# Result rows 4 partitions apart, one output DMA, stationary operands padded to 32 columns: a decode block on one core

## The chip, the cores and the metric

The kernel runs on one core of a Trainium2 chip. The metric is the device time of an execution in microseconds (us); the tables quote medians. The profile is one execution taken by the hardware profiler; its span is about 2.1 us shorter than the time quoted.

## The reference

The block is one decode step for 8 sequences of width 512. It attends over the last 1024 positions of a key/value cache (32 query heads, 8 key/value heads of 128), runs a gated FFN, and gates the attention result with it.

```
xn = layernorm(x)                                    # x: 8 x 512, bf16
q  = xn @ wq;  k, v = last 1024 rows of the caches
s  = softmax(q k^T / sqrt(128)) v  @ wo              # 8 x 512
g  = silu((gelu(xn @ w_gate) * (xn @ w_up)) @ w_down)
return x + s * g
```

## The kernel before

All caches and weights, 47.46 MB, are streamed through 21 slots of 1 MB by SyncE's DMA queue. The computation runs under that stream. The result is kept as 128 partitions x 128 columns: column tile q (128 of the 512 columns) lies on partitions 32 q to 32 q + 7, one row per sequence. The four tiles are made by four column groups of TensorE.

```
for q in range(NQ):                                  # residual, 4 loads of 2 KB
    nc.scalar.dma_start(out=xq_sb[32*q : 32*q+B, :], in_=x_flat[:, q*P : (q+1)*P])
...
nc.vector.memset(s_ps, 0.0)
...
def project_out(m):
    for e in range(HS):
        for q in range(NQ):
            nc.tensor.matmul(s_ps[32*q : 32*q+B, :], oE[m][:, e, :],   # 8 columns
                             wo_t[m][:, e, q*P : (q+1)*P], ...)
...
for m in range(NM):
    project_out(m)
nc.vector.tensor_tensor(out=tmp, in0=s_ps, in1=g_sb, op=ALU.mult)
nc.vector.tensor_tensor(out=out_sb, in0=tmp, in1=xr_sb, op=ALU.add)
for q in range(NQ):                                  # result, 4 stores of 2 KB
    eng = nc.sync if q % 2 == 0 else nc.scalar
    eng.dma_start(out=out_flat[:, q*P : (q+1)*P], in_=out_sb[32*q : 32*q+B, :])
```

The framework gives each DMA one of eight semaphores, taken in turn over all queues (called HW0 to HW7 here). A DMA waits until the previous user of its semaphore has landed.

The softmax here doesn't subtract the row's maximum and nothing guards it: scores larger than these inputs give would overflow.

## Time and profile before

| | before |
|---|---|
| time, median | 123.18 us (123.14 to 123.26, 3 runs) |
| span of the profile | 121.1 us |
| last projection group starts | 116.75 us |
| out_sb ready | 118.44 us |
| fourth output DMA landed | 120.29 us |
| from out_sb to the end of the span | 2.70 us |

These are lines of the page of the kernel before. The DMA row has the busy tenths of the DMA engines in 40 slices of the span. The last line is the share of each engine in the chain of work that ended last.

```profile
span 121.1 us, 4123 instructions
DMA  3999999999999999999999999999999999999820
DMA 82%; PE 12%; DVE 2%; SPq 1%; issue 0%
```

DMA is the limit from slice 2 to slice 37. What comes before the first transfer or after the last one can still give something, and the change acts mostly at the end. The timeline shows the end (start, duration, engine, line, instruction, and in brackets the idle time before it with what ended it); SPq and ACTq are the issuing of DMAs on SyncE and ScalarE.

```profile
116.75 1.02 PE L383 MATMUL s_ps<-slot,oE_2360 128*8 128x128 bf16 x32 [0.88 <-DMA slot<-in_A_wo_dram]
117.82 0.29 DVE L483 TENSOR_TENSOR tmp<-s_ps,g_sb 128x128 f32<-128x128 f32 x1 [7.06 <-PE s_ps L383]
118.14 0.29 DVE L485 TENSOR_TENSOR out_sb<-tmp,xr_sb 128x128 bf16<-128x128 f32 x1
118.47 0.71 SPq L488 DMA_DIRECT2D out_dram<-out_sb  x2
118.47 0.65 ACTq L488 DMA_DIRECT2D out_dram<-out_sb  x2
```

The view of one tile, here the output in DRAM, has the durations of the issues (minimum/median/maximum in ns).

```profile
L488 SPq DMA_DIRECT2D out_dram<-out_sb x2: 298/333/368, 118.5 to 118.9; - x2
L488 ACTq DMA_DIRECT2D out_dram<-out_sb x2: 302/306/309, 118.5 to 118.8; - x2
```

### The profile page before, as it was taken

The numbers are of one execution on the slowest core, as the hardware profiler recorded it, in microseconds if no ns is written. First come the engines' busy times: TensorE is split into PE (matmuls) and PEld (weight loads), VectorE is DVE, ScalarE is ACT, GpSimd is POOL, SyncE is SP. The second block draws the span as 40 slices with busy tenths as digits, with TensorE's granted clock in tenths as the row PEclk, the third lists the DMA queues.
The fourth block names the chain that finished last, engine by engine and source line by source line (L and its number), as shares of the span: only waits on it lengthen the run. The fifth ranks groups of instructions, "written<-read, shape, count | busy, mean of one in ns | idle before, by whom it ended". The sixth has DMA issues, their size and how long they took to land.

```text
span 121.1 us, 4123 instructions
## 1 busy us (share of the span) xinstructions
PE 86.0 (71%) x1856; PEld 71.1 (59%) x1856; DVE 72.3 (60%) x150; ACT 22.6 (19%) x70; POOL 2.4 (2%) x15
## 2 busy tenths in 40 slices
PE   0075269696875968999997969566798789955450
PEld 0061029586865957999896969565698542134340
DVE  2352046866956749678989987747798670562000
ACT  0440000321303301212330330303033300300000
POOL 6100000000000000000000000000000000000000
PEclk9999756999999985559999999999999756995555
DMA  3999999999999999999999999999999999999820
GB/s 84 387 430 430 430 427 417 419 430 425 425 427 427 425 414 422 430 419 430 425 427 422 422 417 430 422 425 422 425 433 418 422 414 434 416 430 423 341 88 5
DMA packets 6929, 47.73 MB, mean 394 GB/s; under 512 B 888, under 2 KB 896, under 8 KB 1920
## 3 DMA queue, kind: packets, MB, share of 16 engines
q1 hardware_dynamic: 6800, 47.46, 93.7%
q8 instruction: 14, 0.23, 0.7%
q10 hardware_dynamic: 112, 0.02, 0.1%
q14 instruction: 3, 0.02, 0.1%
HBM read 47.46 MB, written 0.01 MB: 392 GB/s over the span
## 4 chain that ended last, share of the span: by engine, by line
DMA 82%; PE 12%; DVE 2%; SPq 1%; issue 0%
DMA slot<-in_A_k_cache_dram 44%; DMA slot<-in_B_w_gate_dram 16%; DMA slot<-in_A_wo_dram 15%; DMA slot<-in_A_wq_dram 7%; PE kT_ps L282 7%; PE m_ps L329 2%; PE sc_ps L294 2%; SPq L91 1%; PE s_ps L383 1%; DVE kT L286 1%; PE m_ps L316 1%; DVE sums L318 1%; SPq L103 0%; PE m_ps L370 0%; DVE tmp L483 0%
## 5 line engine op out<-in xcount | busy, mean ns | idle before, releaser
L286 DVE COPY kT<-kT_ps 128x1024 bf16<-128x1024 bf16 x64 | 42.2, 677 | 18.1 <-PE kT_ps L282 17.5
L282 PE MATMUL kT_ps<-ident,slot 128*128 128x128 bf16 x512 | 43.4, 234 | 9.9 <-DMA slot<-in_A_k_cache_dram 9.5
L282 PEld LDWEIGHTS <-slot 128*128 128x128 bf16 x512 | 32.6, 104 | 13.3 <-DMA slot<-in_A_k_cache_dram 10.1
L304 ACT ACTIVATE pT<-sc_ps,diag 128x128 bf16<-128x128 f32 x64 | 18.2, 368 | 70.6 <-PE sc_ps L294 70.6
L294 PE MATMUL sc_ps<-qT_all,kT 128*128 128x16 bf16 x512 | 22.9, 171 | 0.3 <-issue 0.3
L329 PE MATMUL m_ps<-pT,slot 128*128 128x16 bf16 x512 | 21.8, 170 | 1.2 <-issue 1.1
L329 PEld LDWEIGHTS <-slot 128*128 128x128 bf16 x512 | 18.6, 97 | 4.6 <-issue 3.1
L294 PEld LDWEIGHTS <-kT 128*128 128x128 bf16 x512 | 20.4, 99 | 0.0
L318 DVE TENSOR_REDUCE sums<-m_ps 128x16 f32<-128x512 f32 x16 | 10.9, 684 | 1.2 <-PE m_ps L316 1.2
L402 PE MATMUL m_ps<-slot,xpT_sb 128*32 128x512 bf16 x32 | 7.7, 1105 | 0.0
L316 PE MATMUL m_ps<-pT,ones_pp 128*128 128x512 bf16 x16 | 6.7, 416 | 0.7 <-ACT pT L304 0.7
L250 PE MATMUL m_ps<-slot,xnT_sb 128*32 128x512 bf16 x32 | 3.5, 527 | 4.2 <-DMA slot<-in_A_wq_dram 4.2
L234 PE MATMUL m_ps<-ident,xhat 8*128 8x8 bf16 x4 | 0.3, 168 | 7.0 <-DVE xhat L214 7.0
L259 DVE CAST q_sb<-m_ps 128x512 bf16<-128x512 f32 x2 | 1.3, 686 | 6.6 <-PE m_ps L250 6.6
L356 DVE TENSOR_TENSOR wide<-m_ps,hmask 64x1024 bf16<-64x1024 bf16 x4 | 4.9, 1216 | 0.5 <-PE m_ps L352 0.4
L483 DVE TENSOR_TENSOR tmp<-s_ps,g_sb 128x128 f32<-128x128 f32 x1 | 0.3, 292 | 7.1 <-PE s_ps L383 7.1
L250 PEld LDWEIGHTS <-xnT_sb 128*32 128x32 bf16 x32 | 0.8, 101 | 6.2 <-issue 5.8
L322 DVE RECIPROCAL recip<-sums 128x16 f32<-128x16 f32 x16 | 4.0, 253 | 0.6
L234 PEld LDWEIGHTS <-xhat 8*128 8x128 bf16 x4 | 0.2, 102 | 7.0 <-DVE xhat L214 7.0
L402 PEld LDWEIGHTS <-xpT_sb 128*32 128x32 bf16 x32 | 1.7, 117 | 4.3 <-issue 3.4
L338 DVE TENSOR_TENSOR oT_all<-m_ps,recip 128x16 bf16<-128x16 f32 x16 | 3.5, 218 | 0.4 <-PE m_ps L329 0.3
L352 PE MATMUL m_ps<-ident,oT_all 128*64 128x128 bf16 x4 | 1.0, 253 | 2.7 <-DVE sums L318 2.1
(71 smaller groups left out, 33.4 us busy)
## 6 DMA issues: line engine op xcount, KB each, us to landing
slot<-in_A_k_cache_dram SPq DMA_DIRECT2D x16, 1024.0 KB, 19.4
slot<-in_A_v_cache_dram SPq DMA_DIRECT2D x16, 1024.0 KB, 19.7
slot<-in_A_wq_dram SPq DMA_DIRECT2D x4, 1024.0 KB, 8.6
slot<-in_A_wo_dram SPq DMA_DIRECT2D x3, 1024.0 KB, 18.0
slot<-in_B_w_gate_dram SPq DMA_DIRECT2D x2, 896.0 KB, 20.0
slot<-in_B_w_up_dram SPq DMA_DIRECT2D x2, 896.0 KB, 18.9
slot<-in_B_w_down_dram SPq DMA_DIRECT2D x2, 896.0 KB
slot<-in_A_wo_dram SPq DMA_DIRECT2D x1, 768.0 KB, 17.7
```

What stands on the lines that cost most here:

```text
L250: nc.tensor.matmul(q_ps[n][Q * q : Q * (q + 1), :], xnT_sb[:, k, :], wq_t[k][:, hkv * NW : (hkv + 1) * NW], start=(k == 0), stop=(k == NDC ...
L282: nc.tensor.transpose(t_ps[:, c * P : (c + 1) * P], k_t[g][:, cc * Dh : (cc + 1) * Dh], ident)
L286: nc.vector.tensor_copy(out=kT[n], in_=t_ps)
L294: nc.tensor.matmul(sc[g][:, s * CB + c, :], kT[n][:, c * P : (c + 1) * P], qT_all[:, hkv, b0 : b0 + I, :], start=True, stop=True,)
L304: nc.scalar.activation(out=pT[g][:, :, i * rep : (i + 1) * rep], in_=sc[g][:, :, i * rep : (i + 1) * rep], func=ACT.Exp, bias=diag[:, i : ...
L316: nc.tensor.matmul(sums_ps, ones_pp, pT[g], start=True, stop=True)
L318: nc.vector.tensor_reduce(out=sums, in_=sums_ps.rearrange("p c m -> p m c"), axis=AX.X, op=ALU.add)
L322: nc.vector.reciprocal(out=recip[g], in_=sums)
L329: nc.tensor.matmul(oT[g], v_t[g][:, c * Dh : (c + 1) * Dh], pT[g][:, c, :], start=(c == 0), stop=(c == C - 1),)
L338: nc.vector.tensor_tensor(out=oT_all[:, hkv * rep : (hkv + 1) * rep, b0 : b0 + I].rearrange("p j i -> p i j"), in0=oT[g].rearrange("p (i j ...
L356: nc.vector.tensor_tensor(out=wide, in0=t_ps.rearrange("p (q e) -> p e q", e=HS) .unsqueeze(2) .to_broadcast([HS * B, HS, HS, DQ]), in1=hm ...
L402: nc.tensor.matmul(gu_ps[w][Q * q : Q * (q + 1), :], xpT_sb[:, k, :], cols[:, j0[q] : j0[q] + JQ, :], start=(k == 0), stop=(k == NDC - 1), ...
```

## The change

The intent: four output DMAs land one behind the other, so put the 32 result rows at equal distances (sequence b of tile q on partition 32 q + 4 b), where one access pattern reaches them all. For that the stationary operands become 32 columns wide, with zeros between the valid ones. Padded matmuls write all 128 partitions, so two PSUM memsets fall away. The four small loads of the residual become one as well. (The diff is cut: context lines and the old place where oE was made are left out.)

```diff
+    QB = Q // B                                       # 32 // 8 = 4
-    for q in range(NQ):
-        nc.scalar.dma_start(
-            out=xq_sb[32 * q : 32 * q + B, :], in_=x_flat[:, q * P : (q + 1) * P]
-        )
+    nc.scalar.dma_start(out=xq_sb[::QB, :], in_=x_flat.rearrange("b (q n) -> q b n", n=P))
-    nc.vector.memset(s_ps, 0.0)
-        nc.vector.tensor_copy(out=xpT_sb[:, :, 0:B], in_=t[:, 1])
+        nc.vector.tensor_copy(out=xpT_sb[:, :, ::QB], in_=t[:, 1])
+    oE = [persist.tile([P, HS, Q], BF16, name=f"oE{m}") for m in range(NM)]
+    for m in range(NM):
+        nc.gpsimd.memset(oE[m], 0.0)
-        nc.vector.tensor_copy(out=oE[m], in_=e_ps)
+        nc.vector.tensor_copy(out=oE[m][:, :, ::QB], in_=e_ps)
-                    s_ps[32 * q : 32 * q + B, :],
+                    s_ps[Q * q : Q * (q + 1), :],
-        nc.vector.memset(f_ps, 0.0)
-                    f_ps[Q * q : Q * q + B, :],
-                    hT_sb[:, j - j0[r], Q * r : Q * r + B],
+                    f_ps[Q * q : Q * (q + 1), :],
+                    hT_sb[:, j - j0[r], Q * r : Q * (r + 1)],
-    for q in range(NQ):
-        eng = nc.sync if q % 2 == 0 else nc.scalar
-        eng.dma_start(
-            out=out_flat[:, q * P : (q + 1) * P], in_=out_sb[32 * q : 32 * q + B, :]
-        )
+    nc.sync.dma_start(
+        out=out_flat.rearrange("b (q n) -> q b n", n=P), in_=out_sb[::QB, :]
+    )
```

More of the change, by code (lines that the diff above doesn't have):

```diff
@@ L345, in value_block @@
             )
-    oE, wide_t = {}, {}
+    wide_t = {}
+    oE = [persist.tile([P, HS, Q], BF16, name=f"oE{m}") for m in range(NM)]
+    for m in range(NM):
+        nc.gpsimd.memset(oE[m], 0.0)
     def expand_out(m):
@@ L376, in select_out @@
             )
-        oE[m] = persist.tile([P, HS, B], BF16, name=f"oE{m}")
-        nc.vector.tensor_copy(out=oE[m], in_=e_ps)
+        nc.vector.tensor_copy(out=oE[m][:, :, ::QB], in_=e_ps)
     def project_out(m):
```

## The prediction

> **What bounds the kernel now.** The stream of weights and caches. The 40-slice table shows DMA at nine tenths from slice 2 to 37, at about 425 GB/s; the chain that ended last is 82% DMA, 12% PE, 2% DVE. Only what comes before the first transfer or after the last one can shorten the 121.1 us span. The timeline of the end: the last wo piece lands and starts the last 32 output-projection matmuls at 116.75 us; DVE's tmp starts at 117.82, out_sb ends at 118.44; four 2 KB output DMAs are issued, two on SP (the second at 118.88) and two on ACT, each 0.3 to 0.37 us. The trace's semaphore events show them landing one behind the other: the first complete by 119.68, the second by 119.89, the third by 120.09, the fourth by 120.29. About 0.8 us of closing barrier follows.
>
> **What the change does.**
>
> 1. Output: four DMAs become one. The first of the four needed 1.21 us from issue to landing; the fourth came 0.61 us later, about 0.2 us per DMA, whichever queue issued them. (The Trainium skill, "DMA: Bandwidth & Descriptors", section "Issuing engines are not separate DMA queues", says the queues share the same 16 engines; the trace agrees.) The same page, section "Why a DMA increments its semaphore by 16 and not by 1", says that the slowest dimensions of both patterns decide how many engines work. The old DMAs used 8 (ACT's queue has 112 packets: seven DMAs of 8 data and 8 semaphore packets); the new one, 4 x 8 rows, should use 4, each with 8 rows in series. A 256-byte packet took 15 to 21 ns, so I add 7 x 18 = 0.13 us, and up to 0.1 us for a longer issue. Estimated landing: about 119.85, 0.35 to 0.5 us earlier, all on the critical path.
>
> 2. Stationary operands of 32 columns instead of 8, in both down projections (output, FFN). In the last group the matmuls start in bursts of four, 107 ns apart at the halved clock; their weight loads start within 10 ns and lie under the running burst. Single loads took 82 ns (8 columns) and 92 ns (32 columns, query projection). I expect the spacing to remain 107 ns, and under 0.05 us of critical path. Earlier groups have over 1.4 us of slack (waits on wo).
>
> 3. Removed: two PSUM memsets on DVE (0.17 us each). Added: four GpSimd memsets (estimated 0.3 us each, GpSimd idle). Changed: a strided oE copy (0.21 us). All off the path.
>
> 4. Input: four xq DMAs (1.37 us on ACT's queue) become one, so the Sqrt and the first PE work come up to 1 us earlier. DMA semaphores come from a pool of eight taken in turn; three fewer early users let the fourth wq load and K's second load issue without waiting. But the DMA share is already about 1 from 3 us on, so a deeper queue moves 0 to 0.1 us.
>
> **Sum.** 123.18 - 0.4 gives 122.8 us, range 122.4 to 123.2. Faster by over 2%: 0.01; within 2%: 0.98; slower: 0.01.
>
> **What would show it.** One output issue on SP, out_sb's end to span end about 2.25 us instead of 2.65; the last projection group still 1.02 us; the last wo wait ending near 116.7; wq issues in one run at the start.
>
> **What would make it wrong.** The four-engine write costing more; 32-column loads spreading the bursts (up to +0.5 us); the last transfers, where throughput falls to about 150 GB/s from 115 to 116.75 us because some engines lag, ending at another time because of the changed early queue.

## More of the kernel before

At the end SyncE waits for the last count of every semaphore, in a fixed order: HW2; HW3 and HW1; HW4 and HW0; HW5; HW6; HW7, each of the last three together with an engine's semaphore. Then come a drain and a barrier.

The view of waits on SyncE's queue says for how long its closing list waited for outputs (total, times, longest):

```profile
SPq L516 <- DMA out_dram<-out_sb: 0.7, 3, 0.4
```

## The result, and the profile after

| | before | after |
|---|---|---|
| time, median | 123.21 us (4 runs) | 123.88 us (123.84 to 123.92, 4 runs) |
| ratio | | 1.0055 (95% interval 1.0038 to 1.0072) |
| span | 121.1 us | 121.8 us |
| last projection group starts | 116.75 us | 116.73 us |
| out_sb ready | 118.44 us | 118.44 us |
| last output landing | 120.29 us | 120.26 us |
| from out_sb to the end of the span | 2.70 us | 3.34 us |

A ratio is the mean time of one kernel's fast runs over that of the other's of the same rounds, so it is not quite the ratio of the medians quoted. The result is within 2%, and clearly slower by 0.5%. It lies outside the predicted range of 122.4 to 123.2 us.

The page after, same three lines as before:

```profile
span 121.8 us, 4119 instructions
DMA  3999999999999999999999999999999999999710
DMA 93%; SPq 2%; PE 1%; issue 0%; DVE 0%
```

The timeline of the end, the tile view of the output, and the wait of the closing list:

```profile
116.73 1.04 PE L384 MATMUL s_ps<-slot,oE 128*32 128x128 bf16 x32 [0.99 <-DMA slot<-in_A_wo_dram]
117.82 0.29 DVE L483 TENSOR_TENSOR tmp<-s_ps,g_sb 128x128 f32<-128x128 f32 x1 [7.27 <-PE s_ps L384]
118.14 0.29 DVE L485 TENSOR_TENSOR out_sb<-tmp,xr_sb 128x128 bf16<-128x128 f32 x1
118.46 0.69 SPq L486 DMA_DIRECT2D out_dram<-out_sb  x1
```

```profile
L486 SPq DMA_DIRECT2D out_dram<-out_sb x1: 689/689/689, 118.5 to 118.5; - x1
```

```profile
SPq L514 <- DMA out_dram<-out_sb: 1.0, 1, 1.0
```

From the start of the last projection group (116.75 and 116.73 us) to out_sb (118.44 us) the two traces agree to 0.02 us. Earlier stages differ (the FFN's down projection starts at 108.52 and 107.75 us), but all wait for the same stream. The whole difference, 0.64 us of the span, comes after the last computing instruction. The single issue takes 0.69 us where the first one took 0.37, and only one wait for an output remains.

These views do not show what SyncE does after that wait. The trace's records of SyncE's own instructions and of the semaphore events do. "n" is the place of the instruction among all of SyncE's in the trace, "gap" the time since the end of the one ahead:

```
before                                        after
 n  start    gap ns  waits for                 n  start    gap ns  waits for
78  119.219     45   HW2                       77  119.209     56   HW2
79  119.278     42   HW3, HW1                  78  119.268     42   HW3, HW1 (output; held to 120.281)
80  119.726    420   HW4, HW0 (output)         79  120.324     43   HW4, HW0
81  119.903    149   HW5 (output)              80  120.795    443   HW5
82  120.106    175   HW6 (output)              81  120.879     56   HW6
83  120.308    174   HW7 (output)              82  120.949     42   HW7
84  120.378     42   drain                     83  121.021     44   drain
output landings: 119.68 119.89 120.09 120.29   output landing: 120.26
```

Before, the outputs happen to signal on HW4 to HW7, the end of the list, and SyncE drains 0.09 us after the last landing. After, three fewer loads at the start have turned the pool of semaphores, and the output signals on HW1, in the second wait. Four more waits follow the landing, with a pause of 0.44 us before the 80th instruction although what it waits for landed long ago. The drain comes 0.76 us after the landing. From drain to the end of the span it is about 0.76 us in both kernels (121.14 - 120.38; 121.78 - 121.02).

The sum: the landing came 0.03 us earlier, the path from landing to drain grew by 0.67 us (0.76 - 0.09), together 0.64 us, which is the difference of the spans.

### The profile page after: what moved, and what is told of

Same layout as the page of the kernel before. It is cut to its first block, busy times and chain, and to the rows that moved or that the text cites. A ratio compares the mean times of both kernels' runs of the same rounds, so it can differ in the third digit from the quotient of the medians.

```text
span 121.8 us, 4119 instructions
## 1 busy us (share of the span) xinstructions
PE 87.1 (72%) x1856; PEld 71.6 (59%) x1856; DVE 72.6 (60%) x148; ACT 22.6 (19%) x70; POOL 3.4 (3%) x19
## 4 chain that ended last, share of the span: by engine, by line
DMA 93%; SPq 2%; PE 1%; issue 0%; DVE 0%
DMA slot<-in_A_k_cache_dram 62%; DMA slot<-in_B_w_gate_dram 16%; DMA slot<-in_A_wo_dram 15%; SPq L106 2%; PE s_ps L384 1%; SPq L94 1%; DVE tmp L483 0%; DVE out_sb L485 0%; SPq L137 0%; SPq L113 0%
## 5 line engine op out<-in xcount | busy, mean ns | idle before, releaser
L249 PE MATMUL m_ps<-slot,xnT_sb 128*32 128x512 bf16 x32 | 4.2, 618 | 4.3 <-DMA slot<-in_A_wq_dram 4.3
L384 PE MATMUL s_ps<-slot,oE 128*32 128x128 bf16 x128 | 4.2, 309 | 4.2 <-DMA slot<-in_A_wo_dram 4.2
L384 PEld LDWEIGHTS <-oE 128*32 128x32 bf16 x128 | 3.5, 138 | 4.9 <-issue 4.9
```

What stands on the lines that cost most here:

```text
L249: nc.tensor.matmul(q_ps[n][Q * q : Q * (q + 1), :], xnT_sb[:, k, :], wq_t[k][:, hkv * NW : (hkv + 1) * NW], start=(k == 0), stop=(k == NDC ...
L384: nc.tensor.matmul(s_ps[Q * q : Q * (q + 1), :], oE[m][:, e, :], wo_t[m][:, e, q * P : (q + 1) * P], start=(m == 0 and e == 0), stop=(m == ...
```

## The experiments

Three theories: C, the loss is in the closing list; D, the single 32-row DMA is slow in itself; P, padding costs time. A fourth, S (the partition step makes the issue slow), came out of the first runs. Every kernel but the probe was timed in five rounds beside the kernel before on the same chip; all gave a correct result. Intervals are 95%. "Tail" is the time from the end of out_sb to the end of the span in the trace of that run.

### pad_only: both DMA merges undone

```diff
-    nc.scalar.dma_start(out=xq_sb[::QB, :], in_=x_flat.rearrange(...))
+    for q in range(NQ):
+        nc.scalar.dma_start(out=xq_sb[Q*q : Q*(q+1) : QB, :], in_=x_flat[:, q*P : (q+1)*P])
-    nc.sync.dma_start(out=out_flat.rearrange(...), in_=out_sb[::QB, :])
+    for q in range(NQ):
+        eng = nc.sync if q % 2 == 0 else nc.scalar
+        eng.dma_start(out=out_flat[:, q*P : (q+1)*P], in_=out_sb[Q*q : Q*(q+1) : QB, :])
```

> The changed kernel with both DMA merges undone: four input loads of the residual and four output DMAs, rows still 4 partitions apart, 32-column stationaries and the new memsets kept. Theory C (closing waits: the loss lies in SyncE's list of semaphore waits after the output has landed, and in nothing before it): as before, 123.2 us, closing drain of SyncE about 0.09 us after the last output landing. Rival P (padding, memsets or strided writes cost the 0.7 us): 123.8.

Measured: 123.94 us, ratio 1.0067 (1.0055 to 1.0080). Theory C missed; the number is the one rival P gave, but not its reason. The last projection group took 1.04 us, as after, and started at 116.68. The tail was 3.72 us, 1.02 us longer than before (the time grew by less, 0.78 us; most of the rest lies outside the span, see the last experiments), and the tile view of the output shows where that came from:

```profile
L491 SPq DMA_DIRECT2D out_dram<-out_sb x2: 726/760/795, 118.4 to 119.3; - x2
L491 ACTq DMA_DIRECT2D out_dram<-out_sb x2: 647/670/692, 118.4 to 119.2; - x2
```

The same four stores of 8 rows as before, now read from every fourth partition, take 0.65 to 0.80 us each to issue instead of 0.30 to 0.37. The fourth landed 2.87 us after out_sb instead of 1.85. The drain again followed the last landing by 0.09 us, as the outputs were back on HW4 to HW7. So a second cost was in the change: theory S.

### before_x3: the kernel before, with its output semaphores turned by three

```diff
+    scratch = persist.tile([B, 3, P], BF16, name="scratch")
+    for i in range(3):
+        nc.scalar.dma_start(out=scratch[:, i, :], in_=wo_t[NM - 2][0:B, i, 0:P])
     tmp = small.tile([P, P], FP32, name="tmp")
```

> The kernel before, untouched but for three 2 KB copies SBUF to SBUF on ScalarE's DMA queue just before the end, read from a piece of wo that landed at about 114.8 us. They only turn the pool of eight DMA semaphores by three, so that the last output DMA signals on the one that SyncE waits for first instead of last. Theory C: the outputs land at the same time (about 1.85 us after out_sb), then all other closing waits follow one by one, with a pause of about 0.43 us among them: 0.7 us slower than before, 123.9. Rival D (the single 32-row DMA itself is slow, the waits are harmless): 123.2.

Measured: 123.89 us, ratio 1.0061 (1.0048 to 1.0073). In its timeline SyncE's two output issues take the same 0.71 us together as before:

```profile
118.41 0.71 SPq L491 DMA_DIRECT2D out_dram<-out_sb  x2
```

The waits of SyncE's queue:

```profile
SPq L519 <- DMA out_dram<-out_sb: 1.1, 1, 1.1
```

The last output landed 1.83 us after out_sb, against 1.85 before. SyncE then needed 0.84 us from that landing to its drain instead of 0.09, with 0.44 us of it before its 80th instruction. Nothing about the output DMAs had changed, so theory C holds: the kernel before becomes as slow as the changed one when its last output signals first in the list.

### one_out_x6 and two_out_x5: the output moved to the end of the list with extra copies

one_out_x6 is the changed kernel with six such copies; two_out_x5 has five and two output DMAs of 16 rows:

```diff
+    out_r = out_flat.rearrange("b (q n) -> q b n", n=P)
+    for i, eng in enumerate((nc.sync, nc.scalar)):
+        eng.dma_start(out=out_r[2*i : 2*i+2], in_=out_sb[2*Q*i : 2*Q*(i+1) : QB, :])
```

> The changed kernel with six such copies, which put its single output DMA on the semaphore that SyncE waits for last. Theory C: landing 1.8 us after out_sb as in the changed kernel, drain 0.09 us later: 123.15 us (0.7 below the changed kernel, equal to before within 0.1). Rival D: as the changed kernel, 123.9.

> The changed kernel with two output DMAs of 16 rows, one on SyncE and one on ScalarE, and five copies so that they signal on the last two semaphores of the list. Theory C with the issue cost read from the traces (8 rows 0.30 to 0.37 us, 32 rows 0.69 us): issue about 0.45 us, the second lands about 1.5 us after out_sb, 0.3 us before the fourth of the four: 122.9 us. If landing depends on the rows in all and not on how they are split: 123.15.

Measured: both 123.41 us, ratios 1.0018 and 1.0022 (upper ends 1.0032 and 1.0035). In one_out_x6 the pause stood before the 80th instruction and ended before the output landed, so it cost nothing, and the drain came 0.09 us after the landing: that part of theory C holds. But the landing came 2.01 us after the issue began, not 1.80. The copies were not neutral: each took 0.63 us to issue, so the last was still being issued at 119.07 us. In two_out_x5 the issues took 0.68 and 0.60 us with 16 rows, where I had put 0.45; the second landed 2.05 us after issue. So splitting saved nothing beside one_out_x6, which had copies in flight too (from out_sb to the last landing 2.08 us, 2.04 there), and the issue does not grow with the rows (8 rows took 0.65 to 0.80 us in pad_only).

### one_out_last: the same without extra copies

```diff
-        load_wo(m, cut=HS if m < NM - 1 else HS - 2)
+        load_wo(m, cut=HS - 2)                       # every wo load in two pieces
-    nc.scalar.dma_start(out=xq_sb[::QB, :], in_=...)
+    (four input loads, as in pad_only)
```

> The changed kernel with its single output DMA, put on the semaphore that SyncE waits for last, this time without extra copies: four input loads, and every wo load cut in two (no byte more). Theory C: issue 0.69 us, landing about 1.80 us after issue starts, drain 0.09 us later: 123.15 to 123.25 us. SyncE then has six instructions more before its closing list, so the pause of 0.44 us, which stood before the 80th SyncE instruction in every run so far, should stand before the first wait of the list. Rival (the pause belongs to the fourth wait of the list): it stands there.

Measured: 123.02 us, ratio 0.9986 (0.9972 to 0.9999), a little better than expected (the spans of its five runs, 121.1 to 121.4 us, are not shorter than the 121.0 to 121.3 us of the kernel before beside it; see the last experiments). The single output DMA took 0.695 us to issue and landed 1.81 us after the issue began, as in the changed kernel, and the drain came 0.08 us later; the tail was 2.68 us. The tile view, and SyncE's wait:

```profile
L489 SPq DMA_DIRECT2D out_dram<-out_sb x1: 695/695/695, 118.6 to 118.6; - x1
```

```profile
SPq L517 <- DMA out_dram<-out_sb: 0.4, 1, 0.4
```

Three more SyncE instructions ahead of the list (90 in the trace instead of 87; the six of the expectation was a miscount, though the place it named was right) moved the pause: it was 0.45 us before the first wait of the list, again the 80th instruction of the engine. So the pause belongs to a place in SyncE's program and not to a certain wait (the probe below has it between two DMA issues). What SyncE does in it stays open. One record bears on it: in all fourteen traces an 8 KB packet of kind "instruction" (queue q14) starts 0.62 to 0.95 us after the pause has ended, also in the probe, where the pause comes 45 us later than in the others. That fits a fetch of instructions, but no run tests it. Theory D is right that the single DMA is slow in itself, and wrong that this is the loss: with the same slow DMA the span is 121.2 us, within 0.1 us of the kernel before, and not 121.8.

### contig_four: padding alone, rows on neighbouring partitions

Against pad_only:

```diff
-        nc.vector.tensor_copy(out=xpT_sb[:, :, ::QB], in_=t[:, 1])
+        nc.vector.tensor_copy(out=xpT_sb[:, :, 0:B], in_=t[:, 1])
-        nc.vector.tensor_copy(out=oE[m][:, :, ::QB], in_=e_ps)
+        nc.vector.tensor_copy(out=oE[m][:, :, 0:B], in_=e_ps)
-            in_=out_sb[Q*q : Q*(q+1) : QB, :],
+            in_=out_sb[Q*q : Q*q+B, :],               # the residual's loads likewise
```

> Padding alone: 32-column stationaries, no PSUM memsets, GpSimd memsets of oE as in the changed kernel, but the valid rows stay on 8 neighbouring partitions (32 q + b), and four DMAs each carry input and output as before. Theory S (in pad_only the cost came from reading rows 4 partitions apart: issues of 0.65 to 0.80 us instead of 0.30 to 0.37): issues again 0.30 to 0.37 us, 123.2 us, as before. Rival P (padding itself makes the end late): 123.9 as pad_only.

Measured: 122.83 us, ratio 0.9971 (0.9959 to 0.9984). The issues of the output are back:

```profile
L491 SPq DMA_DIRECT2D out_dram<-out_sb x2: 298/330/363, 118.3 to 118.7; - x2
L491 ACTq DMA_DIRECT2D out_dram<-out_sb x2: 302/306/309, 118.3 to 118.6; - x2
```

The tail is 2.71 us (2.70 before). Rival P falls: padding does not lengthen the end. pad_only differs from this kernel only in the partition step of the rows, and is about 1% slower (1.0067 against 0.9971, each against the kernel before). The 0.3% below before was not expected; it lies outside the span, see contig_again.

### contig_two: two DMAs of 16 neighbouring partitions

An attempt to beat both. With the valid columns at 24 to 31 for even tiles and 0 to 7 for odd ones, tiles 0 and 1 lie on partitions 24 to 39.

```diff
+    OFF = Q - B                                       # 24
-    oE = [persist.tile([P, HS, Q], ...)]
+    oE = [persist.tile([P, HS, Q + OFF], ...)]        # valid at OFF:Q
-                    oE[m][:, e, :],
+                    oE[m][:, e, OFF * (q % 2) : OFF * (q % 2) + Q],
-    nc.sync.dma_start(out=out_flat.rearrange(...), in_=out_sb[::QB, :])
+    for i, eng in enumerate((nc.sync, nc.scalar)):
+        eng.dma_start(out=out_r[2*i : 2*i+2], in_=out_sb[2*Q*i+OFF : 2*Q*i+OFF+2*B, :])
     (the FFN operand and the residual likewise; wo loads cut in two)
```

> A version meant to beat both: operands padded so that the rows of column tiles 0 and 1 lie on partitions 24 to 39, those of 2 and 3 on 88 to 103; two output DMAs of 16 neighbouring partitions, one from SyncE, one from ScalarE, on the last two semaphores of the list; wo loads cut in two, three input loads. If the issue cost hangs on the partition step alone (theory S): issue 0.33 to 0.45 us, second landing 1.4 to 1.5 us after out_sb instead of 1.83: 122.8 us. If it hangs on having more than one row dimension: issue 0.65 us, 123.2.

Measured: 123.25 us, ratio 1.0005 (0.9992 to 1.0018).

```profile
L492 SPq DMA_DIRECT2D out_dram<-out_sb x1: 786/786/786, 118.4 to 118.4; - x1
L492 ACTq DMA_DIRECT2D out_dram<-out_sb x1: 668/668/668, 118.4 to 118.4; - x1
```

Neighbouring partitions alone do not make the issue short: the DRAM side steps in two dimensions (tile, sequence), and the issue is as long as with a partition step, as the second half of the expectation had it. The tail was 2.99 us.

### probe: the issue cost by itself

```diff
+    for step in (1, 2, 4, 8, 16):
+        nc.scalar.dma_start(out=out_flat[:, 0:P], in_=out_sb[0 : step*B : step, :])
+    for step in (1, 2, 4):
+        nc.scalar.dma_start(out=out_r, in_=out_sb[0 : step*32 : step, :])
+    nc.scalar.dma_start(out=out_r[0:2], in_=out_sb[0:16, :])
     (the same eight as loads, one SBUF to SBUF copy; all twice)
```

> The kernel before, with a chain of small DMAs on ScalarE's queue put before its last output DMAs, each waiting for the one ahead, twice over: stores from 8 partitions 1, 2, 4, 8 and 16 apart, from 32 partitions 1, 2 and 4 apart, from 16 neighbours; the same for loads; one SBUF to SBUF copy. Only the issue times and landings are read. Theory S: issue near 0.3 us for step 1 and near 0.65 us for every other step, whatever the number of rows. If rows count: 32 rows step 1 near 0.6 us.

Measured (184 us; only these DMAs are read; both repetitions):

| DMA of 256-byte rows | issue, ns | issue begun to landed, us |
|---|---|---|
| store, 8 rows, step 1 | 306, 478 | 1.22, 1.37 |
| store, 8 rows, step 2 | 769, 699 | 1.83, 1.76 |
| store, 8 rows, step 4 | 648, 641 | 1.70, 1.70 |
| store, 8 rows, step 8 | 614, 599 | 1.68, 1.67 |
| store, 8 rows, step 16 | 597, 590 | 1.65, 1.64 |
| store, 32 rows (4 x 8 in DRAM), step 1 | 677, 670 | 1.83, 1.82 |
| store, 32 rows (4 x 8 in DRAM), step 4 | 552, 552 | 1.70, 1.70 |
| store, 16 rows (2 x 8 in DRAM), step 1 | 650, 652 | 1.75, 1.75 |
| load, 8 rows, step 1 | 439, 438 | 1.48, 1.51 |
| load, 8 rows, step 4 | 662, 662 | 1.99, 1.85 |
| SBUF to SBUF, 8 rows, step 1 | 702, 702 | 1.75, 1.75 |

Theory S holds for 8 rows and is too narrow for 32: step 1 does not help there, as the DRAM side then has two row dimensions. Short issues (0.31 to 0.48 us) were those with neighbouring partitions and a single row step in DRAM; all others took 0.54 to 0.77 us, the seven forms that the table leaves out included. The number of rows made no difference to the landing: 8 rows at step 4 and 32 rows at step 4 both landed 1.70 us after the issue began. The steps always ran in the same order, so the smaller differences between them are not read; and the 32-row store that took 0.55 us here on ScalarE took 0.69 on SyncE in the changed kernel. Of the big loads of the kernel before, some fit: a wo load (128 rows, one row dimension) issues in 0.33 us, a K or V load (sequence and row) in 0.53 to 0.65. Others do not: the first three wq loads, of the form of a wo load, took 0.41 to 0.60 us between 1.5 and 3.2 us (the fourth, at 5.9 us, took 0.33), and the load of x, 8 neighbouring rows, took 0.58. So the form is not the only thing that sets the issue time. In this trace SyncE's 80th instruction is an output DMA that stands right behind another one, and the pause, 0.44 us, is there too.

### before_again, contig_again, pad_wo, pad_wd

```diff
 pad_wo, against the kernel before:
-    nc.vector.memset(s_ps, 0.0)
+    oE = [persist.tile([P, HS, Q], ...)]              # zeroed by GpSimd, valid at 0:B
-                    s_ps[32*q : 32*q+B, :],
+                    s_ps[Q*q : Q*(q+1), :],
 pad_wd, against the kernel before:
-        nc.vector.memset(f_ps, 0.0)
-                    f_ps[Q*q : Q*q+B, :],
-                    hT_sb[:, j - j0[r], Q*r : Q*r+B],
+                    f_ps[Q*q : Q*(q+1), :],
+                    hT_sb[:, j - j0[r], Q*r : Q*(r+1)],
```

These ask whether contig_four's 0.3% is real and which half of the padding gives it. before_again is the kernel before; contig_again is contig_four with a blank line; pad_wo pads the output projection alone, pad_wd the FFN's down projection alone.

> The kernel before against itself, to size what two submissions of one program differ by: ratio 1.000 within 0.1%, and a last projection group that starts at 116.75 us give or take 0.15 in the trace (the range over the runs so far).

> contig_four once more, beside the kernel before against itself. contig_four had measured 0.3% below before with the same tail after out_sb (2.71 us against 2.70), so the gain would have to lie in the stream ahead. If it is a property of the program: ratio 0.996 to 0.998 again. If it was the chip or the hour: 1.000.

> Only the output projection padded to 32 columns (oE zeroed by GpSimd, no memset of its PSUM tile), all else as before. Nothing that the traces show on the critical path changes: 123.2 us. If contig_four's 0.3% is real and comes from this half: 122.85.

> Only the FFN's down projection padded to 32 columns (no memset of its PSUM tile), all else as before. This stage ends 1 us or more before the last wo pieces land: 123.2 us. If contig_four's 0.3% comes from this half: 122.85.

Measured ratios: 1.0002 (0.9990 to 1.0014); 0.9983 (0.9971 to 0.9996); 0.9995 (0.9983 to 1.0007); 0.9997 (0.9985 to 1.0009). contig_four's program was below the kernel before, by 0.2 to 0.3%, and neither half alone was. All four tails are 2.69 to 2.71 us, so the gain is not at the end. The start of the last projection group does not show it either: 116.71 us in before_again, 116.84 in contig_again, 116.56 in contig_four. The spans tell where the gain is: not in the span at all. contig_four's are 121.0 to 121.2 us and contig_again's 121.1 to 121.3, the kernel before beside them 121.0 to 121.3. What is shorter is the time outside the span: 1.71 to 1.87 us in every run of contig_four, contig_again, contig_two, one_out_last and pad_only, and 1.75 in one of the six of pad_wo, against 1.95 to 2.17 us in all other runs. The profile does not cover it, so its cause stays open. By time contig_four is the lowest, by span it is level with the kernel before.

## Why the prediction was wrong, point by point

- **Bounded by the stream, and only the end can change: right.** From the last projection group to out_sb the traces agree to 0.02 us. Both the expected gain and the actual loss lie in the last 3.3 us.
- **The step that failed is step 1, "Estimated landing: about 119.85, 0.35 to 0.5 us earlier, all on the critical path".** Two of its terms were wrong.
  - *The single DMA's own time.* I took 1.21 us from a store of 8 neighbouring rows and added 0.13 us for rows in series and "up to 0.1 us for a longer issue". The issue was 0.32 us longer (689 against 368 ns), and issue to landing took 1.80 us. The cost is not in rows but goes with the form of the access pattern (probe: 8 and 32 rows at step 4 both 1.70 us; 8 neighbouring rows 1.22 to 1.37); why such a pattern is slow no run shows. This ate the gain: landed 0.03 us earlier instead of 0.35 to 0.5.
  - *What follows the landing.* I wrote "about 0.8 us of closing barrier follows" as if it were a constant. It was 0.85 us before and 1.52 after, as four waits and a pause of 0.44 us of SyncE, hidden under the output's flight before, now came behind the landing. before_x3 gives the kernel before the same loss without touching its output DMAs; one_out_last takes it from the changed kernel.
- **The cause of the second term stood in step 4 of the prediction.** It says that the semaphores are a pool of eight taken in turn, and that three fewer early users shift the turns. I asked what that does to the early loads (nothing, as said) and not what it does to the last DMA.
- **The number of engines: right.** One sentence of the Trainium skill, "DMA: Bandwidth & Descriptors", section "Why a DMA increments its semaphore by 16 and not by 1", gave 8 engines before and 4 after. The traces show 8 and 4 single landings per output DMA, and 2 for the 2 x 8 rows of two_out_x5. It was not what mattered.
- **32 columns are nearly free: right.** In the last group four of the seven spacings between bursts of four matmuls were 106 to 107 ns in both traces; the seventh burst came 0.04 us after the very last piece of wo had landed (117.32 us before, 117.30 after), so that landing paces the end of the group too. The group took 1.04 us instead of 1.02. The FFN's down projection took 1.68 us instead of 1.12, but at a granted clock of 0.50 instead of 0.78 in those stretches, and it ended before the next wo landing in both. The spans of contig_four and the two halves, 121.0 to 121.3 us, confirm it.
- **Memsets, copies and early work off the path: right.** The four GpSimd memsets took 0.30 us each, as estimated (in the trace before, GpSimd zeroed a tile of half the size in 0.20 us). The first matmul came 0.74 us earlier (6.22 against 6.96 us) and the wq loads were issued in one run, and neither moved the end.
- **What the merge is worth.** one_out_last, whose last output is again last in the closing list, gives what the merge itself is worth: a tail of 2.68 us against 2.70. The expected 0.4 us was never there to be had with this access pattern.

## What to carry to other kernels

Merging small DMAs at the end of a kernel pays only if the merged pattern issues as fast as the small ones: in these runs a step between partitions or a second row dimension cost about 0.3 us of issue and 0.5 us up to landing, as much as the queueing that it was to save. Look at what the program does after its last landing: where DMAs take their semaphores in turn, adding or removing any of them can change on which one the last signals, and here its place in the closing list was worth 0.7 us, while the merge itself saved 0.02. Compare spans as well as times: here 0.3 us of time lay outside the span. When an experiment misses, compare it with the kernel that differs from it in one property (here contig_four against pad_only) before believing a rival whose number happens to fit.

## What the Trainium skill lacked or had wrong

- "DMA: Bandwidth & Descriptors", section "Rules for kernel authors", advises to coalesce many small transfers into one large one. For 32 rows of 256 bytes the one transfer landed 0.03 us earlier than the last of four; the page gives no issue time for Trainium2 by form of pattern. Measured in the probe: 0.31 to 0.48 us for neighbouring partitions with one DRAM row step, 0.54 to 0.77 us for a partition step, two row dimensions, or SBUF to SBUF (at the start of the kernel before, the simple form took up to 0.60 us too).
- No page tells of the closing list of semaphore waits: 0.09 us from the last landing to the drain when the last output's semaphore is last in it, 0.76 to 0.84 us when it is first or second.
- No page that I found gives the pause of 0.44 to 0.46 us before SyncE's 80th instruction, seen in the trace of the changed kernel and in those of all twelve experiments, at whatever that instruction was. The gap of 0.42 us in the trace of the kernel before stands at the same place, mixed with a landing. An 8 KB instruction packet starts 0.62 to 0.95 us after it in every trace.
- "SBUF — State Buffer", section "SBUF: two separate sides", says that a GpSimd operation and a VectorE operation of certain kinds lock a shared port pair against each other for a whole instruction. The changed kernel fits that in kind: while its four oE memsets ran (3.50 to 4.56 us), an 8-column VectorE copy took 1.15 us instead of 0.16. But the copy had begun at 3.44 us, before the first of them, and ended only after the fourth, so one instruction's lock alone does not account for it; the trace does not show which kind the copy was, and no run isolates it. It cost nothing here.
